# Half-height products side by side in a block's first product, and a planned first exchange, in a routed mixture of experts

## The chip, the core and the metric

The kernel runs on one core of one Trainium2 chip. The metric is the device time of one execution in microseconds (us), taken as the median of several runs; lower is better. TensorE (PE in the profile) multiplies, VectorE (DVE) and ScalarE (ACT) do element-wise work, GpSimd (POOL) and SyncE (SP) issue the transfers. A matmul needs its stationary operand loaded first, by an instruction of its own (LDWEIGHTS, PEld in the profile).

## What is computed

A causal convolution of 7 taps a head over 8 x 3584 tokens of 192 numbers, then a mixture of 8 experts in which each of the N = 28672 tokens goes to the one expert with the highest logit:

```python
x = _attn_ref(x, weight).reshape(B * S, D)          # D = 192
xn = x / (np.linalg.norm(x, axis=-1, keepdims=True) + 1e-06)
en = emb / (np.linalg.norm(emb, axis=-1, keepdims=True) + 1e-06)
logits = xn @ en.T / tau
expert_idx = np.argmax(logits, axis=1)
gate_w = softmax(logits)[np.arange(N), expert_idx]
for e in range(8):
    mask = expert_idx == e
    h = np.maximum(x[mask] @ w1[e], 0.0)            # 192 -> 1024
    out[mask] = gate_w[mask, None] * (h @ w2[e])    # 1024 -> 192
```

## The kernel before

Numbers are held as two f16 parts, a high one and a low one, and a product is the sum of high x high, low x high and high x low.

**The head** (`head`, planned by `_Plan`) loads and splits the weights of the eight experts (`weights`, where `low` on DVE writes the low parts, line L437, from what `high` on ACT wrote, L432), convolves and routes the first two chunks of 1792 tokens and convolves the third (`chunk`, line L529). `_Plan` is a list scheduler: `P.add(engine, us, emit, *after)` adds a step with a guessed duration, and `run` emits the steps in the order of the earliest possible start. What it emits on PE, DVE and ACT keeps that order. A step's `lag` is added for a follower on another engine.

**Routing.** The other chunks are convolved (`mix`, L761), routed (`route`) and their rows scattered to per-expert lists in DRAM, piece by piece in between the blocks (`dispatch`, driven by `run`). `run` holds the next piece in `live`; it is None once every chunk has been routed.

**Blocks** (`expert`). A block is up to 512 tokens of one expert, fetched transposed (`fetch`, a DMA into `e_xT`, and a small one into `e_mt`). The 192 inputs stand in `e_xT` as three groups of 128 rows: k = 0 the high parts of inputs 0 to 127, k = 2 their low parts, and k = 1 the high parts of inputs 128 to 191 on rows 0 to 63 and their low parts on rows 64 to 127. The exchange (`flip`, L1128, two DVE copies into `e_xf`) makes from k = 1 a group k = 3 whose halves are swapped. `copy_w1` (L1088) and `copy_w2` (L1091) copy the block's weights into `slot`.

The first product (L1161) makes 8 chunks of 128 hidden values. A bank of the accumulator holds m = 512 / T chunks of a block of T tokens, so T = 512 takes 8 banks, T = 256 takes 4 and T = 128 takes 2. Each chunk takes five whole matmuls:

```python
for i, (o, k) in enumerate(
        ((0, 0), (0, 2), (1, 0), (2, 1), (2, 3))):
```

Here o names the weights: 0 and 1 the high and low ones for inputs 0 to 127, 2 both parts for inputs 128 to 191, which stand high over low for the first four chunks and low over high for the last four. The pair (2, 1) and (2, 3) together gives the three wanted products of inputs 128 to 191 and one more, low x low. Each finished bank is read by ACT (L1165, relu, the high part `hh`) and then by DVE (L1167, the low part `hl`). The second product (L1189) takes 24 matmuls of 192 columns for every 128 tokens, then ACT scales the result (L1194) and POOL scatters it to the output (L1196).

The eight banks are in three rings, `h` with 5, `r` with 2 and `l` with 1; both products use `h`, and the other two serve the routing. The scheduler of the framework may reorder instructions where no dependency holds them; `_dep(..., False)` pins an order without a wait.

Of the kernel before, what the change touches and what calls it, by code (L numbers as in the profile page):

```python
# [40 lines left out]
NFC = F // 128  # L41
# [21 lines left out]
LATE = 1.0  # L63
PICKED = 5.0
ACTS = 8, 10, 16
LAND_X, LAND_T = 9.0, 6.0
TURN, FETCH, PIECE = 5.1, 2.1, 1.4
RANK_L, RANK_P = 2.0, 1.5
STEP1, STEP2, STEPC, STEPL = 1.08, 1.98, 0.65, 0.62
# [63 lines left out]
def _dep(tc, frm, to, sync=True):  # L133
    cls = mybir.DependencyClass.Sync if sync else mybir.DependencyClass.NoSync
    tc.add_manual_dep(
        frm, to, mybir.DependencyInfo(cls, mybir.DependencyReason.DATA),
        reason="routed rows are written before they are read",
    )


class _Moe:
    def __init__(self, ctx, tc, x, weight, emb, tau, w1, w2, out):
# [38 lines left out]
        self.xts, self.mixed = [], {}  # L181
        self.clk, self.gated, self.mm = 0.0, False, None
        self.asked, self.sp_at, self.low, self.parts = {}, 0.0, None, []
        self.chosen = {}
        self.subs, self.ready, self.flips, self.at, self.copied = [], 0, 0, 0, 0


    def ps(self, ring, shape, dt, name):
        n = 2048 // (2 if dt == F16 else 4)
        t = self.rings[ring].tile([128, n], dt, tag=ring, name=name)  # L190
        w = int(np.prod(shape[1:]))
        v = t[: shape[0], :w]
        if len(shape) == 3:
            v = v.rearrange("p (a b) -> p a b", b=shape[2])
        elif len(shape) == 4:
            v = v.rearrange("p (a b c) -> p a b c", b=shape[2], c=shape[3])
        return v
# [941 lines left out]
    def expert(self):  # L1139
# [13 lines left out]
            "p (c t) -> p c t", t=T) for i in range(2))  # L1153

        m = 512 // T
        for b in range(0, NFC, m):
            ps = self.ps("h", [128, m, T], F32, "h_ps")
            for c in range(m):
                for i, (o, k) in enumerate(
                        ((0, 0), (0, 2), (1, 0), (2, 1), (2, 3))):  # L1160
                    self.mm = nc.tensor.matmul(  # L1161
                        out=ps[:, c, :], lhsT=w1(o, b + c), rhs=xk[k],
                        start=(i == 0), stop=(i == 4)).ins
                    self.tick(STEP1 / (5 * m), self.mm)
            self.step = nc.scalar.activation(  # L1165
                out=hh[:, b:b + m, :], in_=ps, func=AF.Relu).ins
            self.low = nc.vector.scalar_tensor_tensor(  # L1167
                out=hl[:, b:b + m, :], in0=ps, scalar=0.0, in1=hh[:, b:b + m, :],
                op0=ALU.max, op1=ALU.subtract).ins
            if b == (0 if m > 2 else 2 if m == 2 else 1) and u == 0:  # L1170
                self.copy_w2()
            if m == 4:
                self.copy_w1(self.at, (b // 4,))
            yield self.slack(512)
# [5 lines left out]
            scalar1=self.slot[:, WS:RES].bitcast(F32), scalar2=None, op0=ALU.mult)  # L1180
        terms = sum(([(hh, c, k) for c in range(b, b + m) for k in (0, D)]
                     + [(hl, c, 0) for c in range(b, b + m)]
                     for b in range(0, NFC, m)), [])
        for a in range(nj):
            self.next_out = self.clk + STEP2 + EVICT
            o = self.ps("h", [128, D], F32, "o_ps")
# [73 lines left out]
    def head(self, first):  # L1260
# [35 lines left out]
            self.subs += sum(self.pick(128, first, most=MORE), [])  # L1296

        n = p = P.add("DVE", 3.8, pick, ranked[-1], pri=PICKED)
        for _ in range(3):
            n = P.add("SP", 2.0, lambda: self.fetch(), n, *sent, at)  # L1300
        n = P.add("DVE", 1.3, lambda: self.copy_w1(0), p,
                  *[v for l in low for v in l[:3]])
        P.add("DVE", 4.2, more, n, *[l[3] for l in low], pri=2.0)
        P.run()
        self.asked = {c: -LAND_X for c in range(4)}
        self.sp_at = 0.0
# [37 lines left out]
    def run(self):  # L1344
# [21 lines left out]
        while live or self.pend or not done or self.at < len(self.subs):  # L1366
# [16 lines left out]
            else:  # L1383
# [2 lines left out]
                self.clk += 0.5  # L1386
                if live:
                    live = next(a, None)
            if not live and not done and not self.pend:
                self.last_blocks()  # L1390
                done = True
# [27 lines left out]
```

## Time and profile before

| what | value |
|---|---|
| median of 3 runs | 1187.54 us (1187.27 to 1188.91) |
| profiled execution, its own time | 1184.81 us |
| profiled execution, span first to last instruction | 1183.1 us |
| PE busy | 1118.7 us, 95% of the span |
| DVE, ACT, POOL busy | 73%, 50%, 46% |
| mean granted clock of TensorE | 0.965 |

The 1.7 us between the span and its execution's time lie around the instructions. Matmuls are pipelined: a record's end is modelled and reaches past the start of the next one, so the cost of a matmul in a stream is read from start to start. The granted clock is 1.0 at 2.4 GHz and 0.5 at 1.2 GHz.

### The profile page before, as it was taken

How to read it: one execution, taken by the hardware profiler on the slowest of the kernel's cores; microseconds unless marked ns; L12 is line 12 of the kernel's file. 1: busy time of each engine (PE TensorE's matmuls, PEld its weight loads, DVE VectorE, ACT ScalarE, POOL GpSimd, SP SyncE). 2: the span in 40 equal slices, each digit the busy share in tenths (PEclk: the TensorE clock that was granted, in tenths of full speed). 3: DMA queues.
4: the chain of work that ended last, by engine and by line, in shares of the span. 5: the costliest groups of instructions: out<-in, count | busy, mean ns of one | idle time of the engine just before them, and what ended most of it. 6: DMA issues, size and time to landing. Idle time of an engine off the chain costs nothing. (4 is left out here: it accounts for less than half of the span.)

```text
span 1183.1 us, 29407 instructions
## 1 busy us (share of the span) xinstructions
PE 1118.7 (95%) x10732; PEld 911.5 (77%) x10732; DVE 866.3 (73%) x2314; ACT 592.3 (50%) x1354; POOL 546.5 (46%) x538
## 2 busy tenths in 40 slices
PE   5736999999999999999999999999999999999998
PEld 3633887889888898678967676776677777889997
DVE  5996998787978889768797676755447456467775
ACT  5867856364635546456464554434433334333333
POOL 1273245747555574655756556465552222222222
PEclk9556999999999999999999999999999999999999
DMA  9762355747365474764754756353222112112220
GB/s 276 232 217 53 81 109 131 164 96 160 74 149 135 116 166 98 156 133 94 176 111 125 147 112 122 79 124 80 70 70 56 39 45 53 44 42 48 49 49 28
DMA packets 267365, 127.50 MB, mean 108 GB/s; under 512 B 208671, under 2 KB 257182, under 8 KB 267217
## 3 DMA queue, kind: packets, MB, share of 16 engines
q1 hardware_dynamic: 243536, 78.71, 31.6%
q0 software_dynamic: 23664, 46.87, 13.9%
q8 instruction: 86, 1.41, 0.5%
q14 instruction: 63, 0.51, 0.2%
q10 hardware_dynamic: 16, 0.01, 0.0%
HBM read 38.35 MB, written 47.24 MB: 72 GB/s over the span
## 5 line engine op out<-in xcount | busy, mean ns | idle before, releaser
L1161 PE MATMUL h_ps<-e_xT,slot 128*128 128x256 f16 (+2 forms) x3136 | 496.5, 290 | 5.1 <-DVE slot L1088 4.8
L1189 PE MATMUL o_ps<-slot,hid 128*128 128x192 f16 x5472 | 481.8, 246 | 3.3 <-DVE hid L1167 2.2
L1189 PEld LDWEIGHTS <-hid 128*128 128x128 f16 x5472 | 453.7, 98 | 31.8 <-issue 9.4
L1161 PEld LDWEIGHTS <-slot 128*128 128x128 f16 x3920 | 345.5, 98 | 157.9 <-issue 10.9
L1196 POOL DMA_INDIRECT out_dram<-y,e_mt x228 | 252.7, 1108 | 437.2 <-ACT y L1194 409.7
L1167 DVE SCALAR_TENSOR_TENSOR hid<-h_ps,hid 128x512 f16<-128x512 f32 x456 | 309.2, 686 | 112.9 <-ACT hid L1165 110.7
L1165 ACT ACTIVATE hid<-h_ps 128x512 f16<-128x512 f32 x456 | 269.1, 597 | 199.3 <-PE h_ps L1161 192.1
L972 POOL DMA_INDIRECT rows_d<-rows,di x256 | 277.3, 1083 | 144.9 <-PE h_ps L1161 40.0
L1194 ACT ACTIVATE y<-o_ps,g 128x192 f32<-128x192 f32 x228 | 95.0, 420 | 305.8 <-PE o_ps L1189 271.6
L1161 PE MATMUL h_ps<-e_xf,slot 128*128 128x256 f16 (+2 forms) x784 | 217.8, 291 | 0.0
L1091 DVE COPY slot<-res 128x3074 f16 x98 | 96.6, 986 | 131.2 <-PE o_ps L1189 125.8
L1088 DVE COPY slot<-res 128x3072 f16 (+1 forms) x119 | 96.4, 810 | 1.2 <-issue 0.6
L761 PE MATMUL conv_ps<-xt,band 128*112 128x384 f32 x208 | 84.5, 498 | 0.0
L766 ACT COPY xt<-conv_ps 112x384 f32<-112x384 f32 x104 | 49.3, 479 | 31.5 <-PE conv_ps L761 30.8
L1128 DVE COPY e_xf<-e_xT 64x256 f16<-64x256 f16 (+2 forms) x196 | 46.1, 235 | 17.7 <-DMA e_xT<-rows_d 13.6
L773 ACT ACTIVATE sq<-xt 112x192 f32<-112x192 f32 x156 | 55.5, 361 | 1.8 <-DVE sq L777 0.7
L808 ACT CAST rows<-xt 112x768 f16<-112x768 f32 x56 | 46.1, 832 | 11.7 <-DVE xt L806 4.5
L806 DVE TENSOR_TENSOR xt<-xt,x_p_s 112x768 f32<-112x768 f32 x56 | 51.6, 950 | 0.2
L843 PEld LDWEIGHTS <-xT 128*112 128x112 f16 x672 | 44.0, 132 | 7.8 <-DMA xT<-rows 3.1
L843 PE MATMUL lg_ps<-ma,xT 128*112 128x16 f16 x448 | 43.8, 193 | 2.1 <-DMA xT<-rows 1.8
L810 DVE TENSOR_TENSOR rows<-xt,rows 112x512 f16<-112x512 f32 x56 | 38.4, 686 | 5.8 <-ACT rows L808 5.6
L843 PE MATMUL lg_ps<-mb,xT 128*112 128x16 f16 x224 | 37.7, 196 | 0.3 <-ACT xT L838 0.3
(212 smaller groups left out, 644.2 us busy)
## 6 DMA issues: line engine op xcount, KB each, us to landing
xt<-in_dram SPq DMA_DIRECT2D x42, 384.0 KB
res<-in_dram SPq DMA_DIRECT2D x6, 768.0 KB
rows_d<-rows,di POOLq DMA_INDIRECT x256
out_dram<-y,e_mt POOLq DMA_INDIRECT x228
xT<-rows SPq DMA_TRANSPOSE x208
res<-in_dram SPq DMA_DIRECT2D x6, 512.0 KB
xt<-in_dram SPq DMA_DIRECT2D x2, 1536.0 KB
xt<-in_dram SPq DMA_DIRECT2D x2, 1440.0 KB
```

The costliest lines, as they stand in the source:

```text
L761: i = nc.tensor.matmul(out=ps, lhsT=self.band[:, h, :], rhs=xt[:, :, h * G:(h + 1) * G], start=True, stop=True).ins
L773: self.over(nc.scalar.activation(out=sq, in_=xc[:, t, :], func=AF.Square, accum_out=n2[:, t:t + 1]).ins)
L843: i = nc.tensor.matmul(out=lg[:, g * GX + a, :], lhsT=xT[:, a, k, :], rhs=self.mb if k == 1 else self.ma, start=(k == 0), stop=(k == 2)).ins
L972: i = self.nc.gpsimd.indirect_dma_start(out=self.rows_d[:, :], out_offset=bass.IndirectOffsetOnAxis(ap=idx, axis=0), in_=src, in_offset=No ...
L1088: self.under(nc.vector.tensor_copy(out=o, in_=v).ins)
L1091: self.nc.vector.tensor_copy(out=self.slot[:, W2:], in_=self.res2[:, bass.ds(self.we, IMG)])
L1161: self.mm = nc.tensor.matmul(out=ps[:, c, :], lhsT=w1(o, b + c), rhs=xk[k], start=(i == 0), stop=(i == 4)).ins
L1165: self.step = nc.scalar.activation(out=hh[:, b:b + m, :], in_=ps, func=AF.Relu).ins
L1167: self.low = nc.vector.scalar_tensor_tensor(out=hl[:, b:b + m, :], in0=ps, scalar=0.0, in1=hh[:, b:b + m, :], op0=ALU.max, op1=ALU.subtrac ...
L1189: self.mm = nc.tensor.matmul(out=o, lhsT=h[:, c, q], rhs=w2[:, c, k:k + D], start=(n == 0), stop=(n == 3 * NFC - 1)).ins
L1194: self.step = nc.scalar.activation(out=y, in_=o, func=AF.Copy, scale=g[:, a:a + 1]).ins
L1196: i = nc.gpsimd.indirect_dma_start(out=self.out[:, :], out_offset=bass.IndirectOffsetOnAxis(ap=mt[:, a, 0:1], axis=0), in_=y, in_offset=No ...
```

## The change

It has two parts.

**Half-height products.** Once `live` is None (`routed`), blocks of 512 and 256 tokens take four whole matmuls a chunk, of which the fourth is (2, 3) for the first four chunks and (2, 1) for the last four; it gives low x high and high x low of inputs 128 to 191. What is left, high x high, is a matmul of 64 rows: for a chunk of the first half on rows 0 to 63 (`e_xT`), for one of the second half on rows 64 to 127 (`e_xf`). `sides` issues these in pairs, one of each half, into two banks. All pairs of a block stand together behind the first two banks' whole matmuls (behind the first bank's at T = 256), and open the remaining banks. The banks are taken in the order first half, second half, and so are the terms of the second product. `ps` now gives out all eight banks in turn, and each matmul of these blocks is pinned behind the one before (`mul`). The program has 14 such blocks of 512 tokens and 8 of 256, with 56 and 32 pairs. Blocks of 128 tokens, and all blocks before, keep five matmuls a chunk.

**The first exchange.** In `head` the exchange of block 0 becomes a step of the plan, behind `copy_w1` and all low parts of the weights, with a lag of 3.0 us behind the first fetch; `more`, the selection of three small blocks, comes behind it.

```diff
-LAND_X, LAND_T = 9.0, 6.0
+LAND_X, LAND_T, LAND_E = 9.0, 6.0, 3.0
...
     def ps(self, ring, shape, dt, name):
         n = 2048 // (2 if dt == F16 else 4)
+        if self.routed and ring == "h":
+            self.bank += 1
+            ring = "hhrhhrhl"[self.bank % 8]
...
+        order = range(0, NFC, m)
+        if self.routed and m <= 2:
+            order = [v for b in range(0, NFC // 2, m) for v in (b, b + NFC // 2)]
+        banks, half = {}, NFC // 2
+
+        def mul(b, c, o, x, p=slice(0, 128), start=False, stop=False):
+            i = nc.tensor.matmul(
+                out=banks[b][:, c, :], lhsT=w1(o, b + c)[p], rhs=x[p],
+                start=start, stop=stop, skip_group_check=True).ins
+            if self.mm is not None:
+                _dep(tc, i, self.mm.name, False)
+            self.mm = i
+            self.tick(STEP1 / (5 * m), i)
...
+        def full(b):
+            new = b not in banks
+            if new:
+                bank(b)
             for c in range(m):
                 for i, (o, k) in enumerate(
-                        ((0, 0), (0, 2), (1, 0), (2, 1), (2, 3))):
...
+                        ((0, 0), (0, 2), (1, 0), (2, 3 if b < half else 1))):
+                    mul(b, c, o, xk[k], start=new and not c and not i,
+                        stop=not new and i == 3)
+
+        def sides():
+            old = set(banks)
+            for b in range(0, half, m):
+                for v in (b, b + half):
+                    if v not in old:
+                        bank(v)
+                for c in range(m):
+                    for v, k, p in ((b, 1, slice(0, 64)),
+                                    (b + half, 3, slice(64, 128))):
+                        mul(v, c, 2, xk[k], p, start=v not in old and not c,
+                            stop=v in old and c == m - 1)
+
+        for n, b in enumerate(order):
+            if self.routed and m <= 2:
+                if n < 2 // m:
+                    full(b)
+                    if n < 2 // m - 1:
+                        continue
+                    sides()
+                    ready = order[:n + 1]
+                else:
+                    full(b)
+                    ready = [b]
...
+        fetched = []
         for _ in range(3):
-            n = P.add("SP", 2.0, lambda: self.fetch(), n, *sent, at)
+            n = P.add("SP", 2.0, lambda: self.fetch(), n, *sent, at, lag=LAND_E)
+            fetched.append(n)
         n = P.add("DVE", 1.3, lambda: self.copy_w1(0), p,
                   *[v for l in low for v in l[:3]])
-        P.add("DVE", 4.2, more, n, *[l[3] for l in low], pri=2.0)
+        n = P.add("DVE", 0.5, self.flip, n, fetched[0], *[l[3] for l in low])
+        P.add("DVE", 4.2, more, n, pri=2.0)
         P.run()
...
                 if live:
                     live = next(a, None)
+            self.routed = not live
```

The order of the built programs shows three places. In the changed file the lines are shifted: L437 is L440, L1088 is L1091, L1091 is L1094, L1128 is L1131, L1189 is L1244; the whole matmuls of the changed blocks, their pairs and their LDWEIGHTS all have line L1165, that of `mul`.

**DVE at the end of the head, before.** `res_94` and `res_95` hold the experts' weights, `slot` and `hid` as sources the raw weights of the last two experts.

```order
L437 SCALAR_TENSOR_TENSOR res_94<-slot,w_p_s,res_94 128x1024
L1128 COPY e_xf<-e_xT 64x256 x2
L437 SCALAR_TENSOR_TENSOR res_94<-slot,w_p_s,res_94 64x512 x2
L437 SCALAR_TENSOR_TENSOR res_94<-hid,w_p_s,res_94 128x1024
L437 SCALAR_TENSOR_TENSOR res_94<-hid,w_p_s,res_94 64x512 x2
L1076 TENSOR_LOAD sel_3584_989
L1088 ISA
L1088 COPY slot<-res_94 128x3072
L437 SCALAR_TENSOR_TENSOR res_95<-slot,w_p_s,res_95 128x8x192
L437 SCALAR_TENSOR_TENSOR res_95<-hid,w_p_s,res_95 128x8x192
L1007 TENSOR_TENSOR sl_av<-cb_871,start 1x8
```

The same place now:

```order
L440 SCALAR_TENSOR_TENSOR res_94<-slot,w_p_s,res_94 128x1024
L440 SCALAR_TENSOR_TENSOR res_94<-slot,w_p_s,res_94 64x512 x2
L440 SCALAR_TENSOR_TENSOR res_94<-hid,w_p_s,res_94 128x1024
L440 SCALAR_TENSOR_TENSOR res_94<-hid,w_p_s,res_94 64x512 x2
L1079 TENSOR_LOAD sel_3584_989
L1091 ISA
L1091 COPY slot<-res_94 128x3072
L440 SCALAR_TENSOR_TENSOR res_95<-slot,w_p_s,res_95 128x8x192
L440 SCALAR_TENSOR_TENSOR res_95<-hid,w_p_s,res_95 128x8x192
L1131 COPY e_xf<-e_xT 64x256 x2
L1010 TENSOR_TENSOR sl_av<-cb_871,start 1x8
```

The exchange (COPY e_xf, two copies in one row) has moved from behind the first low part of expert 6 to behind the last low part of expert 7; five low parts, the copy of block 0's first weights and the two 128x8x192 low parts now stand ahead of it.

**PE in the first product of a routed 512 block, before.** h_ps_13393, 13401 and so on are banks in turn, e_xT and e_xf the block's inputs.

```order
L1161 MATMUL h_ps_13393<-e_xT_12909,slot_96 128x512
L1161 LDWEIGHTS slot_96
L1161 MATMUL h_ps_13393<-e_xT_12909,slot_96 128x512
L1161 LDWEIGHTS slot_96
L1161 MATMUL h_ps_13393<-e_xf_13347,slot_96 128x512
L1161 LDWEIGHTS slot_96
L1161 MATMUL h_ps_13401<-e_xT_12909,slot_96 128x512
L1161 LDWEIGHTS slot_96
L1161 MATMUL h_ps_13401<-e_xT_12909,slot_96 128x512
L1161 LDWEIGHTS slot_96
```

The same block now, from the last whole matmul of the second bank on; 13393 and 13398 are the first two banks, for chunks 0 and 4.

```order
L1165 MATMUL h_ps_13398<-e_xT_12909,slot_96 128x512
L1165 LDWEIGHTS slot_96
L1165 MATMUL h_ps_13393<-e_xT_12909,slot_96 128x512
L1165 LDWEIGHTS slot_96
L1165 MATMUL h_ps_13398<-e_xf_13347,slot_96 128x512
L1165 LDWEIGHTS slot_96
L1165 MATMUL h_ps_13406<-e_xT_12909,slot_96 128x512
L1165 LDWEIGHTS slot_96
L1165 MATMUL h_ps_13407<-e_xf_13347,slot_96 128x512
L1165 LDWEIGHTS slot_96
L1165 MATMUL h_ps_13410<-e_xT_12909,slot_96 128x512
L1165 LDWEIGHTS slot_96
```

The last two matmuls of before into one bank have become one whole matmul, and pairs of e_xT and e_xf into two banks each follow each other; the rows don't say that they are of 64 rows.

**PE from a 128 block into a 256 block, before.** o_ps_16959 is the 128 block's second product, of 24 matmuls; h_ps_17005 and 17018 are the first banks of the 256 block.

```order
L1189 MATMUL o_ps_16959<-slot_96,hid_99 128x192
L1161 LDWEIGHTS slot_96
L1161 MATMUL h_ps_17005<-e_xT_16694,slot_96 128x256
L1161 LDWEIGHTS slot_96
L1161 MATMUL h_ps_17005<-e_xT_16694,slot_96 128x256
...
L1161 MATMUL h_ps_17018<-e_xT_16694,slot_96 128x256
L1189 LDWEIGHTS hid_99
L1189 MATMUL o_ps_16959<-slot_96,hid_99 128x192
L1189 LDWEIGHTS hid_99
...
L1161 MATMUL h_ps_17005<-e_xf_16989,slot_96 128x256
```

The same place now:

```order
L1244 LDWEIGHTS hid_99
L1244 MATMUL o_ps_16959<-slot_96,hid_99 128x192
L1165 LDWEIGHTS slot_96
L1165 MATMUL h_ps_17005<-e_xT_16694,slot_96 128x256
L1165 LDWEIGHTS slot_96
L1165 MATMUL h_ps_17005<-e_xT_16694,slot_96 128x256
L1165 LDWEIGHTS slot_96
L1165 MATMUL h_ps_17005<-e_xT_16694,slot_96 128x256
L1165 LDWEIGHTS slot_96
L1165 MATMUL h_ps_17005<-e_xf_16989,slot_96 128x256
L1165 LDWEIGHTS slot_96
```

Before, eight matmuls of the next block that read e_xT stood ahead of the last four of the second product, and e_xf was first read after sixteen matmuls of the block. Now the second product runs through and e_xf is read by the fourth.

## Rows read from the trace of the kernel before

**Rows 1.** The page, part 1: busy time of each engine.

```profile
PE 1118.7 (95%) x10732; PEld 911.5 (77%) x10732; DVE 866.3 (73%) x2314; ACT 592.3 (50%) x1354; POOL 546.5 (46%) x538
```

**Rows 2.** Stages of 20 us: length, busy (x instructions) of PE, PEld, DVE, ACT, POOL, clock, DMA, GB/s.

```profile
120.00:140.00 20.00, 19.60 (x215) 17.15 (x213) 19.68 (x64) 18.14 (x57) 5.84 (x6) 1.00 0.44 90
820.00:840.00 20.00, 20.00 (x154) 13.38 (x153) 10.29 (x17) 8.38 (x16) 10.58 (x12) 1.00 0.29 74
```

**Rows 3.** Waits of PE from 110 us on: total us, times, longest.

```profile
PE h_ps L1161 <- DVE slot L1088: 4.8, 3, 3.5
PE o_ps L1189 <- DVE hid L1167: 2.2, 3, 1.7
```

**Rows 4.** Timeline, end of the head: start, us, engine, what, [idle before it <- releaser].

```profile
94.61 1.28 DVE L437 SCALAR_TENSOR_TENSOR res<-slot,w_p_s,res 128x1024 f16<-128x1024 f32 x1 [0.34 <-ACT res L432]
...
99.96 1.56 ACT L432 ACTIVATE res<-hid,w_p_s 128x1536 f16<-128x1536 f32 x1
...
105.12 0.46 DVE L1128 COPY e_xf<-e_xT 64x256 f16<-64x256 f16 x2 [9.22 <-DMA e_xT<-rows_d]
...
105.50 1.52 DVE L437 SCALAR_TENSOR_TENSOR res<-slot,w_p_s,res 64x512 f16<-64x512 f32 x2
105.91 1.49 PE L761 MATMUL conv_ps<-xt,band 128*112 128x384 f32 x2
...
107.05 2.84 DVE L437 SCALAR_TENSOR_TENSOR res<-hid,w_p_s,res 128x1024 f16<-128x1024 f32 x3
...
109.93 0.96 DVE L1088 COPY slot<-res 128x3072 f16 x1
...
110.94 0.61 PE L1161 MATMUL h_ps<-e_xT,slot 128*128 128x256 f16 x4 [3.55 <-DVE slot L1088]
```

**Rows 5.** Stages of 1 us at the end of the head, columns as in rows 2.

```profile
107.00:108.00 1.00, 0.40 (x1) 0.00 (x0) 0.97 (x2) 1.00 (x6) 0.00 (x0) 0.50 0.37 49
108.00:109.00 1.00, 0.00 (x0) 0.00 (x0) 0.97 (x2) 0.61 (x4) 0.00 (x0) 0.94 0.13 16
...
111.00:112.00 1.00, 1.00 (x8) 0.82 (x9) 1.00 (x1) 0.00 (x0) 0.00 (x0) 0.76 0.03 8
112.00:113.00 1.00, 1.00 (x5) 0.72 (x4) 1.00 (x2) 0.23 (x1) 0.00 (x0) 0.50 0.00 0
...
114.00:115.00 1.00, 1.00 (x7) 0.73 (x5) 1.00 (x3) 0.89 (x4) 0.00 (x0) 0.53 0.00 0
```

**Rows 6.** Timeline of PE in the first routed 512 block, columns as in rows 4.

```profile
798.47 1.03 PE L1161 MATMUL h_ps<-e_xT,slot 128*128 128x512 f16 x4
...
807.10 8.08 PE L1189 MATMUL o_ps<-slot,hid 128*128 128x192 f16 x96
815.02 1.03 PE L1161 MATMUL h_ps<-e_xT,slot 128*128 128x512 f16 x4
```

**Rows 7.** Timeline of PE in a 256 block.

```profile
1155.32 0.60 PE L1161 MATMUL h_ps<-e_xT,slot 128*128 128x256 f16 x4
...
1155.98 0.60 PE L1161 MATMUL h_ps<-e_xT,slot 128*128 128x256 f16 x4
```

**Rows 8.** Groups of instructions by form: busy us, mean ns of one, idle before, releasers.

```profile
L1167 DVE SCALAR_TENSOR_TENSOR hid<-h_ps,hid 128x512 f16<-128x512 f32 x456 | 309.2, 686 | 112.9 <-ACT hid L1165 110.7
...
L1165 ACT ACTIVATE hid<-h_ps 128x512 f16<-128x512 f32 x456 | 269.1, 597 | 199.3 <-PE h_ps L1161 192.1 <-DVE slot L1091 1.0 <-DVE hid L1167 0.7
...
L1091 DVE COPY slot<-res 128x3074 f16 x98 | 96.6, 986 | 131.2 <-PE o_ps L1189 125.8 <-issue 5.2
...
L1161 PE MATMUL h_ps<-e_xf,slot 128*128 128x512 f16 x216 | 79.2, 379 | 0.0
```

**Rows 9.** Timeline from a 128 block into a 256 block.

```profile
1150.14 1.85 PE L1189 MATMUL o_ps<-slot,hid 128*128 128x192 f16 x20
...
1151.15 0.68 DVE L1167 SCALAR_TENSOR_TENSOR hid<-h_ps,hid 128x512 f16<-128x512 f32 x1
...
1152.33 0.46 DVE L1128 COPY e_xf<-e_xT 64x256 f16<-64x256 f16 x2
```

More of the change, by code (lines that the diff above doesn't have):

```diff
@@ L183, in __init__ @@
         self.asked, self.sp_at, self.low, self.parts = {}, 0.0, None, []
-        self.chosen = {}
+        self.chosen, self.routed, self.bank = {}, False, 0
         self.subs, self.ready, self.flips, self.at, self.copied = [], 0, 0, 0, 0
@@ L1155, in expert @@
         m = 512 // T
-        for b in range(0, NFC, m):
-            ps = self.ps("h", [128, m, T], F32, "h_ps")
+        order = range(0, NFC, m)
[10 more added lines that the diff above has]
+            self.tick(STEP1 / (5 * m), i)
@@ L1158, in expert, with bank @@
+        def bank(b):
+            banks[b] = self.ps("h", [128, m, T], F32, "h_ps")
+        def full(b):
+            new = b not in banks
+            if new:
+                bank(b)
             for c in range(m):
                 for i, (o, k) in enumerate(
-                        ((0, 0), (0, 2), (1, 0), (2, 1), (2, 3))):
-                    self.mm = nc.tensor.matmul(
-                        out=ps[:, c, :], lhsT=w1(o, b + c), rhs=xk[k],
-                        start=(i == 0), stop=(i == 4)).ins
@@ L1164, in expert @@
[L1164 to L1170, printed above, removed]
+                        ((0, 0), (0, 2), (1, 0), (2, 3 if b < half else 1))):
@@ new lines, in expert @@
+        for n, b in enumerate(order):
[9 more added lines that the diff above has]
+                    ready = [b]
+            else:
+                bank(b)
+                for c in range(m):
+                    for i, (o, k) in enumerate(
+                            ((0, 0), (0, 2), (1, 0), (2, 1), (2, 3))):
+                        self.mm = nc.tensor.matmul(
+                            out=banks[b][:, c, :], lhsT=w1(o, b + c), rhs=xk[k],
+                            start=(i == 0), stop=(i == 4)).ins
+                        self.tick(STEP1 / (5 * m), self.mm)
+                ready = [b]
+            for v in ready:
+                self.step = nc.scalar.activation(
+                    out=hh[:, v:v + m, :], in_=banks[v], func=AF.Relu).ins
+                self.low = nc.vector.scalar_tensor_tensor(
+                    out=hl[:, v:v + m, :], in0=banks[v], scalar=0.0,
+                    in1=hh[:, v:v + m, :], op0=ALU.max, op1=ALU.subtract).ins
+            if n == (0 if m > 2 else 1) and u == 0:
@@ L1182, in expert @@
                      + [(hl, c, 0) for c in range(b, b + m)]
-                     for b in range(0, NFC, m)), [])
+                     for b in order), [])
         for a in range(nj):
```

## The prediction

> **What bounds the kernel now.** I read the page first: PE is busy 1118.7 of 1183.1 us, the next engine, DVE, 866.3 [rows 1]. A share of the whole span hides stages, so next the stages of 20 us. Just behind the head, from 120 to 140 us, PE is busy 19.60, but DVE 19.68 and ACT 18.14: three engines are close together. Behind all routing, from 820 to 840 us, PE is busy all 20.00 at full clock and DVE only 10.29, ACT 8.38 [rows 2]. There whatever PE is spared should come off the time. Then PE's waits from 110 us on: the longest is 3.5 us, on DVE's copy into slot; the three waits of the second product on DVE's low parts are 2.2 us together [rows 3]. So from the first block on PE waits for little, and in the head it waits for DVE. The timeline of the end of the head says why: DVE has written the first low part of expert 6 at 94.61 + 1.28 = 95.89, and then idles 9.22 us for the landing of e_xT, because the exchange stands next in its order; only behind it come the five low parts that the copy of the first weights needs (1.52 and 2.84 us), then this copy at 109.93, and PE begins block 0 at 110.94, after 3.55 us of waiting for it [rows 4].
>
> **The planned exchange.** It is issued as before, two copies, but behind those parts. DVE goes on at 95.89: two low parts of 1.52 us, then three of 2.84 end at 100.3, the copy of 0.96 at 101.3; ACT's last high part ends at 99.96 + 1.56 = 101.5, so the two 128x1536 low parts end near 105. The row of 105.12 gives the landing: the exchange runs when it did before [rows 4]. So DVE is over 8 us ahead, the exchange is hidden behind nothing but the landing, and what is queued behind it (the selection of `more`, the copy of the second weights) moves forward with it. PE cannot use all that: two convolutions stand ahead of block 0 at 105.91 and their record ends at 107.4 [rows 4]. The first matmuls need e_xT (105.1) and slot (101.3), so they start at about 107.4: 3.55 us.
>
> There is a second gain in the same place. PE's clock reads 0.50 from 107 to 108 and 0.94 in the next us; PE then idles, block 0 starts at full clock at 110.94, and the clock falls to 0.76, 0.50, 0.50 (113 to 114 reads like the one before) and 0.53 in the four stages from 111 us on [rows 5]. The half-clock time in there is 0.48 + 1.00 + 1.00 + 0.94 = 3.4 us, which costs half of it, 1.7. Starting at 107.4, PE has half clock for 0.6 + 0.12 us, a cost of 0.36, and then no idle stretch ahead of a fall. Gain 1.35. Together **-4.9 us**. Bounds: 0, if DVE or ACT bind from 120 us on, and 3.55 + 1.7 = 5.3.
>
> **The half-height products.** In the first routed 512 block the first product runs from 798.47 to 807.10, 8.63 us for 40 matmuls, 0.2157 each; the second 7.92 us for 96 [rows 6]. In a 256 block six matmuls take 1155.98 - 1155.32 = 0.66, 0.11 each [rows 7]. The change leaves 32 whole matmuls and 4 pairs a block. No row shows two matmuls in the array at once. If a pair lasts as long as one matmul, a block of 512 saves 4 x 0.2157 = 0.863, a block of 256 saves 0.44: 14 x 0.863 + 8 x 0.44 = **-15.6 us**. If they run one after the other, a pair costs two and the saving is 0. I take the upper end: the two halves share no rows of the array and no bank, and a load of weights (PEld, 13.38 us busy in a stage where PE is busy 20.00 [rows 2]) fits twice into a pair of 512.
>
> The array has to be divided ahead of the pairs and made whole behind them, twice a block, 44 times. No row shows such a switch. At the lower end it costs nothing. For the price, I take the emptying of the array: a whole 512 matmul has a record of 379 ns [rows 8], but the next starts after 216 [rows 6]; the 163 ns between is what a matmul needs behind its last column. If nothing new enters in that time, 44 x 0.163 = **+7.2 us**. If a load of weights is laid open as well, some 0.1 us more, 11.6; that is the upper end. I take 7.2, the nearest row.
>
> The page "TensorEngine Tiling (Array Packing)" of the Trainium skill states, under Tiling Modes, that a change of the tiling mode, not only of the tile, drains the engine. It speaks against a free switch; no run here has shown it yet. The page "TensorE: Matmul & The Clock Gate", Part 3, gives starts 4 ns apart for matmuls in different row groups, but a measured 3.07 for four. By 3.07 / 4, an estimate, two would gain 1.54 and not 2, and a pair of 512 would last 0.28 us; the saving would be 11.0 in place of 15.6, and the sum -6.0 in place of -10.6. A rival of that kind is priced below, from rows.
>
> **What the fixed order costs.** From a 128 block into a 256 block, before, PE had twelve matmuls to do until the exchange was through. Now the second product runs through: 24 matmuls from 1150.14 at 0.0825 end at 1152.12, three matmuls on e_xT at 1152.45, and the fourth needs e_xf, which DVE finishes at 1152.33 + 0.46 = 1152.79 [rows 6, 7, 9]: 0.34 us of waiting at each of the 8 such blocks, **+2.7 us**. The last four of the 24 need the low part that ends at 1151.83 and start after 20, at 1151.79: nothing to 0.1 us. Bounds 0 and 3.6. Ahead of a 512 block three whole matmuls give 0.3 us more cover than ahead of a 256 one, so I put nothing there.
>
> **What stays hidden.** The copies, exchanges and transfers of a block are the same in number; DVE at 10.29 of 20 hides them. Two banks now are finished at once, behind 8 matmuls and 4 pairs, at 8 x 0.2157 + 0.88 = 2.6 us, the others every 0.863. DVE needs 0.686 a bank, ACT 0.597 [rows 8], so both keep up: the eight low parts end at about 2.6 + 0.6 + 8 x 0.686 = 8.7, or 0.7 + 0.6 behind the last bank at 7.9 with the switches, 9.2; the second product needs the last at 7.9 + 23 x 0.0825 = 9.8. Cover 0.6 us. All banks in turn means that the eighth reuses that of the last second product; it is opened 2.4 us later, and ACT reads it within one.
>
> **Sum.** -4.9 - 15.6 + 7.2 + 2.7 = -10.6 us. Against the profiled execution's own 1184.81 that is 1174.2; that execution was 2.7 us below the median of the runs, 1187.54, and I carry the difference to the median: **1176.9 us**.
>
> **Rivals.** (1) *The pairs run one after the other, and the switches cost.* Place: the eight half-height matmuls of a block. For it: no row shows two at once. Against: separate rows and banks. Then 0 + 7.2 + 2.7 - 4.9 = +5.0, 1192.5, slower. It decides from the point where less than 5.0 of the 15.6 us, a third of each pair's second matmul, is overlapped. (2) *One after the other and free switches*: -2.2, 1185.3. (3) *Pairs side by side and free switches*, the weights and columns of the next mode entering behind the last: -17.8, 1169.7. For it: in the stream, loads of weights already overlap the matmuls. (4) *The head's gain is given back*, because DVE at 19.68 and ACT at 18.14 of 20 [rows 2] bind behind it: -5.7, 1181.8. Against: DVE itself is over 8 us ahead. (5) *DVE becomes late for the second product*: if the copy of the second weights, 0.986 us [rows 8], falls between the low parts and not ahead of them, the cover of 0.6 turns into a wait of 0.4 in each of the 14 blocks of 512, +5.6: -5.0, 1182.5. Against: that copy waits only for the second product before, which has ended when the block begins. (6) *The halves overlap only in part*: the second of a pair starts behind its own load of weights, as the second product seems to run, at 0.0825 a matmul. A pair then lasts 0.298 us at 512 and 0.19 at 256, the saving is 14 x 0.53 + 8 x 0.11 = 8.4, and the sum -3.4, 1184.1. For it: a load stands between the two in the order. Against: in whole matmuls the load is hidden [rows 6].
>
> **Chances.** Forecast 0.46, own range 1173 to 1181 (a pair somewhat longer than one matmul, a switch from 0.07 to 0.25 us). (1) 0.08, (2) 0.06, (3) 0.16, (4) 0.09, (5) 0.06, (6) 0.09. About 0.2%, 2.4 us, can be told from no change here. Faster are the forecast and (3) to (6): 0.86; (2) is within it, 0.06; (1) slower, 0.08. The range 1168 to 1186 takes in all but (1) and the tails of free switches and of a dear one.
>
> **What would show it.** In the changed trace: block 0's first matmul at about 107.4 and no half clock behind 109; the exchange still at 105. In a routed 512 block the start of the first product to that of the second 8.63 - 0.86 + 0.33 = 8.1 us, near 4.1 at 256 for 4.4; in the pairs, records of e_xT and e_xf that start together. A first product of 8.6 or more means rival 1 or 2, of 7.8 rival 3. PE's waits would list e_xf by about 0.3 us eight times, and if rival 5 holds, hid in the second product. The forecast is wrong if PE's start in the head is set by something other than these two convolutions, or if a pair is worth much less than one whole matmul.

## The result, and the profile after

| what | before | after |
|---|---|---|
| median | 1187.4 us (1186.25 to 1188.91, 4 runs) | 1172.32 us (1170.1 to 1173.61, 4 runs) |
| profiled execution, its own time | 1184.81 us | 1172.65 us |
| profiled execution, span | 1183.1 us | 1170.9 us |

The ratio is 0.9868, 95% interval 0.985 to 0.9885: faster, by 15.1 us in the medians (1.3%). The forecast was 1176.9 with a range of 1168 to 1186, so the time lies inside, 4.6 us below the forecast. The narrower range that the prediction gave to its own mechanism, 1173 to 1181, it misses by 0.7 us.

The page, part 1, of the changed kernel answers to [rows 1]; PE has lost 10.4 us of busy time with as many matmuls:

```profile
PE 1108.3 (95%) x10732; PEld 898.3 (77%) x10732; DVE 868.3 (74%) x2314; ACT 592.0 (51%) x1354; POOL 550.0 (47%) x538
```

Two stretches tell where the time went: from the last group of matmuls on the weight totals (`n_ps`, in the head, ahead of both edits) to the first routed block, and from there to the end. Stages of before, columns as in rows 2:

```profile
92.38:798.47 706.09, 692.22 (x6545) 564.62 (x6545) 557.52 (x1594) 381.57 (x958) 390.04 (x371) 0.99 0.55 122
798.47:1183.10 384.63, 378.93 (x3826) 308.56 (x3824) 232.56 (x463) 145.18 (x274) 120.51 (x119) 1.00 0.21 52
```

The same stages of the changed kernel:

```profile
93.98:794.87 700.89, 690.44 (x6545) 564.20 (x6546) 557.79 (x1594) 380.66 (x958) 388.47 (x371) 0.99 0.56 122
794.87:1170.90 376.03, 369.86 (x3826) 295.98 (x3824) 234.35 (x463) 145.81 (x274) 125.60 (x119) 1.00 0.21 53
```

The first stretch is 5.2 us shorter, the second 8.6. What lies ahead of them differs by 1.6 us the other way (93.98 against 92.38), and -5.2 - 8.6 + 1.6 is the 12.2 us between the two profiled executions. That of before was 2.6 us below its median, that of after 0.3 above; the rest of the 15.1 is in there.

The first routed 512 block, PE's timeline of the changed kernel (columns as in rows 4), answers to [rows 6]:

```profile
794.87 0.81 PE L1165 MATMUL h_ps<-e_xT,slot 128*128 128x512 f16 x3
795.51 0.38 PE L1165 MATMUL h_ps<-e_xf,slot 128*128 128x512 f16 x1
795.73 1.35 PE L1165 MATMUL h_ps<-e_xT,slot 128*128 128x512 f16 x5
796.69 0.39 PE L1165 MATMUL h_ps<-e_xf,slot 64*128 64x512 f16 x1
796.92 0.38 PE L1165 MATMUL h_ps<-e_xT,slot 64*128 64x512 f16 x1
796.92 0.38 PE L1165 MATMUL h_ps<-e_xf,slot 64*128 64x512 f16 x1
...
797.35 0.38 PE L1165 MATMUL h_ps<-e_xT,slot 64*128 64x512 f16 x1
797.35 0.38 PE L1165 MATMUL h_ps<-e_xf,slot 64*128 64x512 f16 x1
797.66 0.82 PE L1165 MATMUL h_ps<-e_xT,slot 128*128 128x512 f16 x3
...
802.85 3.38 PE L1244 MATMUL o_ps<-slot,hid 128*128 128x192 f16 x39
```

The two halves of a pair start together (2 to 4 ns apart in each of the 88 pairs of the trace), and the next pair about 0.216 us later (796.69 to 797.35 are three pitches, 0.22 each), as whole matmuls follow one another. The fifth instruction in the row of 795.73 is the first pair's half on e_xT (its record ends where its partner's does, at 797.08). Four whole matmuls from 795.73 would be through at 796.59, but the pair begins at 796.69; the last pair at 797.35 would be through at 797.57, but the next whole matmul begins at 797.66. Those two gaps of about 0.10 us are the switches. The first product is 802.85 - 794.87 = 7.98 us, where it was 8.63 [rows 6]: 36 x 0.2157 = 7.77, and 0.21.

The loads of weights (PEld) in the same place of the changed kernel show what stands in the gaps:

```profile
796.69 0.55 PEld L1165 LDWEIGHTS <-slot 64*128 64x128 f16 x8 [0.42 <-issue]
797.66 4.86 PEld L1165 LDWEIGHTS <-slot 128*128 128x128 f16 x24 [0.42 <-issue]
```

Within a run of whole matmuls a load starts 0.21 us ahead of its own matmul, beside the one before. At a switch it does not: the first load behind each of the 44 switches starts 4 to 5 ns ahead of its matmul, and its record is 92 to 97 ns long, about as long as the gap.

From a 128 block into a 256 block, timeline of DVE and PE of the changed kernel, answers to [rows 9]:

```profile
1152.55 0.49 PE L1165 MATMUL h_ps<-e_xT,slot 128*128 128x256 f16 x3
1152.58 0.46 DVE L1131 COPY e_xf<-e_xT 64x256 f16<-64x256 f16 x2
1153.09 0.27 PE L1165 MATMUL h_ps<-e_xf,slot 128*128 128x256 f16 x1
...
1156.90 0.33 PE L1244 MATMUL o_ps<-slot,hid 128*128 128x192 f16 x2
```

Three matmuls of 0.108 are through at 1152.87, the one on e_xf begins at 1153.09: 0.22 us of waiting for the exchange, which ends at 1153.04. The list of waits does not show it, since the modelled ends of the records cover it; one sees it from start to start only. The first product is 4.35 us. Added up from start to start, those of all 8 such blocks take 34.92 us, before 34.93.

The end of the head in the changed kernel, timeline of all engines, answers to [rows 4]:

```profile
96.21 2.85 DVE L440 SCALAR_TENSOR_TENSOR res<-slot,w_p_s,res 128x1024 f16<-128x1024 f32 x3 [0.34 <-ACT res L435]
98.62 1.25 POOL L975 DMA_INDIRECT rows_d<-rows,di  x1 [0.31 <-issue]
...
101.50 1.55 POOL L975 DMA_INDIRECT rows_d<-rows,di  x1 [0.30 <-issue]
101.97 0.96 DVE L1091 COPY slot<-res 128x3072 f16 x1
...
105.12 1.33 SPq L1109 DMA_TRANSPOSE e_xT<-rows_d  x1
107.15 0.92 PE L764 MATMUL conv_ps<-xt,band 128*112 128x384 f32 x2
108.23 0.45 DVE L1131 COPY e_xf<-e_xT 64x256 f16<-64x256 f16 x2 [1.84 <-DMA e_xT<-rows_d]
108.34 0.92 PE L1214 MATMUL h_ps<-e_xT,slot 128*128 128x256 f16 x7 [0.27 <-DMA e_xT<-rows_d]
```

DVE no longer idles ahead of the low parts, and block 0 begins at 108.34 with a wait of 0.27 for e_xT in place of 3.55 for DVE [rows 4]. Counted from the start of the `n_ps` group (93.98; 92.38 before) it begins after 14.36 us where it was 18.56. The stages of 1 us there, which answer to [rows 5], show that the clock is up when it begins and stays up:

```profile
107.00:108.00 1.00, 1.00 (x3) 0.29 (x1) 0.00 (x0) 0.58 (x2) 0.00 (x0) 0.82 0.78 150
108.00:109.00 1.00, 0.73 (x8) 0.62 (x8) 0.73 (x4) 1.00 (x6) 0.00 (x0) 1.00 0.06 1
...
111.00:112.00 1.00, 1.00 (x8) 0.66 (x7) 0.86 (x7) 1.00 (x6) 0.00 (x0) 1.00 0.17 29
...
114.00:115.00 1.00, 1.00 (x9) 0.63 (x7) 0.40 (x2) 1.00 (x6) 0.00 (x0) 1.00 0.00 0
```

PE's waits from 110 us on, of the changed kernel, answer to [rows 3]: the wait for slot is gone, that for DVE's low parts is 2.6 us in place of 2.2; those for row loads (2.9, where it was 1.8) and for `e_xT` are longer.

```profile
PE lg_ps L846 <- DMA xT<-rows: 2.9, 5, 1.1
PE o_ps L1244 <- DVE hid L1222: 2.6, 4, 1.7
PE h_ps L1214 <- DMA e_xT<-rows_d: 1.0, 1, 1.0
```

### The profile page after: what moved, and what is told of

It is laid out like the page before. It is cut to its first block, busy times and chain, and to the rows that moved or that the text cites. A ratio compares the mean times of both kernels' runs of the same rounds, so it can differ in the third digit from the quotient of the medians.

```text
span 1170.9 us, 29417 instructions
## 1 busy us (share of the span) xinstructions
PE 1108.3 (95%) x10732; PEld 898.3 (77%) x10732; DVE 868.3 (74%) x2314; ACT 592.0 (51%) x1354; POOL 550.0 (47%) x538
## 4 chain that ended last, share of the span: by engine, by line
PE 53%; issue 21%; POOL 9%; DVE 7%; DMA 7%; ACT 2%; SPq 1%; POOLq 0%; DVEq 0%; ACTq 0%
PE h_ps L1214 23%; PE o_ps L1244 20%; POOL out_dram L1251 7%; PE conv_ps L764 5%; PE lg_ps L846 3%; DMA out_dram<-y,e_mt 3%; POOL rows_d L975 2%; DMA xT<-rows 1%; DVE res L440 1%; SPq L971 1%; DMA rows_d<-rows,di 1%; PE conv_ps L532 1%; DMA e_xT<-rows_d 1%; DVE xt L616 1%; DMA band<-cseq_d 0%
## 5 line engine op out<-in xcount | busy, mean ns | idle before, releaser
L1244 PE MATMUL o_ps<-slot,hid 128*128 128x192 f16 x5472 | 480.4, 247 | 3.4 <-DVE hid L1222 2.6
L1244 PEld LDWEIGHTS <-hid 128*128 128x128 f16 x5472 | 453.4, 98 | 30.8 <-issue 9.7
L1214 PE MATMUL h_ps<-e_xT,slot 128*128 128x256 f16 (+2 forms) x2432 | 346.5, 276 | 1.5 <-DMA e_xT<-rows_d 1.3
L1214 PEld LDWEIGHTS <-slot 128*128 128x128 f16 x3040 | 259.4, 98 | 88.5 <-issue 11.4
L1094 DVE COPY slot<-res 128x3074 f16 x98 | 96.5, 985 | 118.2 <-PE o_ps L1244 117.5
L1214 PE MATMUL h_ps<-e_xf,slot 128*128 128x256 f16 (+2 forms) x608 | 164.3, 276 | 0.1
L1165 PE MATMUL h_ps<-e_xT,slot 128*128 128x512 f16 (+3 forms) x704 | 145.7, 341 | 0.0
L1165 PEld LDWEIGHTS <-slot 128*128 128x128 f16 (+1 forms) x880 | 73.4, 97 | 69.6 <-issue 17.5
L1091 DVE COPY slot<-res 128x3072 f16 (+1 forms) x119 | 96.7, 812 | 0.9 <-issue 0.7
L1131 DVE COPY e_xf<-e_xT 64x256 f16<-64x256 f16 (+2 forms) x196 | 46.2, 236 | 9.8 <-DMA e_xT<-rows_d 5.7
L1165 PE MATMUL h_ps<-e_xf,slot 128*128 128x512 f16 (+3 forms) x176 | 48.8, 340 | 0.5
```

Source lines behind the costliest of these rows:

```text
L1091: self.under(nc.vector.tensor_copy(out=o, in_=v).ins)
L1094: self.nc.vector.tensor_copy(out=self.slot[:, W2:], in_=self.res2[:, bass.ds(self.we, IMG)])
L1165: i = nc.tensor.matmul(out=banks[b][:, c, :], lhsT=w1(o, b + c)[p], rhs=x[p], start=start, stop=stop, skip_group_check=True).ins
L1214: self.mm = nc.tensor.matmul(out=banks[b][:, c, :], lhsT=w1(o, b + c), rhs=xk[k], start=(i == 0), stop=(i == 4)).ins
L1244: self.mm = nc.tensor.matmul(out=o, lhsT=h[:, c, q], rhs=w2[:, c, k:k + D], start=(n == 0), stop=(n == 3 * NFC - 1)).ins
```

## The experiments

The theory after this reading: head -5.2 us; pairs -15.6 (they last as one matmul), switches about +4.5 (44 at 0.10), fixed order about +2 in the routed stretch. The main rival: pairs and switches are not two opposite terms, but the new order itself, eight banks in turn and nothing else, is what gains. Each experiment is the changed kernel but for the edit shown. Runs e1 to e4 were timed against a before of 1188.8 us, e5 to e8 against 1189.05. The two stretches of each profiled execution:

| kernel | n_ps to first routed block | from there to the end | median us | ratio to before (95%) |
|---|---|---|---|---|
| before | 706.09 | 384.63 | 1187.4 | |
| changed | 700.89 | 376.03 | 1172.32 | 0.9868 (0.985 to 0.9885) |
| e1, head alone | 701.56 | 384.62 | 1181.95 | 0.9943 (0.9924 to 0.9962) |
| e2, pairs alone | 708.97 | 376.15 | 1179.81 | 0.9921 (0.99 to 0.9942) |
| e3, sides whole | 699.79 | 387.04 | 1182.82 | 0.9951 (0.9932 to 0.9971) |
| e4, split runs | 704.25 | 383.69 | 1182.18 | 0.9936 (0.9913 to 0.9958) |
| e5, e_xf last | 700.61 | 374.27 | 1170.4 | 0.9852 (0.983 to 0.9874) |
| e6, 512 alone | 703.19 | 376.07 | 1173.59 | 0.9873 (0.9853 to 0.9893) |
| e7, early runs | 701.59 | 374.27 | 1169.01 | 0.9834 (0.9814 to 0.9854) |
| e8, early all | 695.58 | 374.22 | 1163.86 | 0.9801 (0.9775 to 0.9826) |

The second column of times moves only with edits to the routed blocks (384.63 and 384.62, 376.03 and 376.15, 374.27, 374.27 and 374.22), so it can be read to 0.1 us. The first cannot. Changed, e1, e3, e4, e5 and e6 have the same program there and spread from 699.79 to 704.25; before and e2, the same as each other, take 706.09 and 708.97. So only the means of such groups tell something: 701.7 with the planned exchange, 707.5 without it. Part of the spread is the clock: near 330 us PE waits for row loads, and then the granted clock reads 0.50 for 3.4 us in six of the ten executions, for 6.8 us in all in e6 and e8, and not at all in e4 and e7, which costs 1.7, 3.4 and 0 us. The stages of 50 us around it in e5, e7 and e8, columns as in rows 2:

```profile
292.89:342.94 50.05, 48.17 (x484) 42.83 (x483) 38.58 (x112) 23.89 (x62) 28.08 (x27) 0.97 0.56 122
292.99:343.11 50.12, 48.15 (x492) 42.68 (x489) 38.32 (x109) 24.60 (x63) 28.39 (x28) 1.00 0.59 121
292.44:342.12 49.68, 46.74 (x460) 39.46 (x459) 36.09 (x106) 22.91 (x60) 29.34 (x26) 0.93 0.54 113
```

**e1, the planned exchange alone.**

```diff
-            self.routed = not live
+            self.routed = False
```

> Only the planned exchange; blocks keep five whole matmuls a chunk and the five h banks. Theory: the exchange alone gives 4.9 to 5.2 us, 1182.3 us; first block's first product about 14.4 us behind the last weight totals' matmul (18.6 before), and 700.9 us from there to the first routed block (706.1 before). Rival: the 5 us were chance of one execution or are given back behind the head, 1187 us.

1181.95 us, 6.9 below before (interval 4.5 to 9.0). The routed stretch is as before:

```profile
92.52:794.08 701.56, 690.75 (x6544) 564.52 (x6545) 557.92 (x1594) 380.98 (x958) 387.75 (x371) 0.99 0.55 122
794.08:1178.70 384.62, 378.93 (x3826) 308.57 (x3824) 232.49 (x463) 145.19 (x274) 120.60 (x119) 1.00 0.21 52
```

The head's gain is there by itself, 4.5 us in the trace, and DVE and ACT don't take it back behind the head (rival 4). Block 0 begins 14.81 us behind `n_ps` here, not 14.4 as expected: the clock is still at 0.50 from 107 to 108, the convolutions take as long as before, and PE begins block 0 behind them without a listed wait:

```profile
107.33 2.34 PE L1214 MATMUL h_ps<-e_xT,slot 128*128 128x256 f16 x16
```

```profile
107.00:108.00 1.00, 1.00 (x5) 0.48 (x4) 0.97 (x3) 1.00 (x6) 0.00 (x0) 0.50 0.25 50
```

**e2, the half-height products alone.** The five lines of the head as in before:

```diff
-        fetched = []
...
-            n = P.add("SP", 2.0, lambda: self.fetch(), n, *sent, at, lag=LAND_E)
-            fetched.append(n)
+            n = P.add("SP", 2.0, lambda: self.fetch(), n, *sent, at)
...
-        n = P.add("DVE", 0.5, self.flip, n, fetched[0], *[l[3] for l in low])
-        P.add("DVE", 4.2, more, n, pri=2.0)
+        P.add("DVE", 4.2, more, n, *[l[3] for l in low], pri=2.0)
```

> Only the half-height pairs; the exchange as before. Theory: the routed stretch is 8.6 us shorter, 1178.8 us, and DVE idles some 9 us again for the landing in the head; the scatters at the end of the head take 0.94 us again as they did before, and not up to 1.55. Rival, most of the gain is in the head: 1183 us or more.

1179.81, 9.0 below before (interval 6.9 to 11.9); 6.85 and 8.99 make 15.8, against 15.1 for both together: the parts add up within their intervals. In its trace block 0 again begins 18.56 us behind n_ps (111.84 - 93.28), after 4.47 us of waiting for slot, with clock 0.50 from 110 to 116:

```profile
111.84 1.03 PE L1214 MATMUL h_ps<-e_xT,slot 128*128 128x256 f16 x4 [4.47 <-DVE slot L1091]
```

Its first stretch is 2.9 us longer than that of before, where the two programs are the same. PE's waits for row loads (`lg_ps` on `xT`) are 5.1 us there, 1.8 in before, enough to account for it.

**e3, the same order with whole sides.** Both matmuls of each pair over all 128 rows, so one after the other and no division of the array. The low x low product comes back, as in before.

```diff
-                    for v, k, p in ((b, 1, slice(0, 64)),
-                                    (b + half, 3, slice(64, 128))):
+                    for v, k, p in ((b, 1, slice(0, 128)),
+                                    (b + half, 3, slice(0, 128))):
```

> The change, but every half-height matmul takes all 128 rows (the fifth product is whole again, low x low comes back), so same order, same eight banks, same pins, no two in the array at once and no switch. Theory: the gain of the routed stretch is the pairs': first product 8.63 us in a 512 block again, total 1184 us (5.2 from the exchange, about 2 lost to the pinned order). Rival: the eight banks and the new order gave the gain, and it stays near 1172 us.

1182.82, and the routed stretch is 387.04: 2.4 us longer than before, not shorter. So the order gains nothing by itself and costs 2.4 (2.7 forecast), and the pairs with their switches are worth 387.04 - 376.03 = 11.0 us. If a pair lasts as one matmul, which the starts above show, that is -15.6, and 4.6 us are left for 44 switches, 0.104 each, the gap seen in the timeline.

**e4, more switches.** The pairs in three runs a 512 block (two pairs, one and one) and in two a 256 block: the same matmuls, and 14 x 4 + 8 x 2 = 72 more switches.

```diff
-        def sides():
+        def sides(at):
             old = set(banks)
-            for b in range(0, half, m):
+            for b in at:
...
-                    sides()
+                    sides([0])
...
+                    if b < half and b:
+                        sides([b])
                     full(b)
```

> The change, but a block's pairs in three runs and not one (two runs at 256 tokens): 72 switches more in all. Theory, each switch costs about 0.1 us: first product 8.4 us in a 512 block for 7.98, total +7.4, 1179.7 us. Rival, the 0.21 us above 36 matmuls are paid once a block (opening banks, waits): 1172 us, first product 8.0.

1182.18, 9.9 above the changed kernel's median. Of that, 1.4 is that the before of these runs was slower; by the two ratios to before it is 8.1. The routed stretch is 383.69, so 7.66 us more than 376.03: 0.106 us a switch, as in e3 and in the gaps. The timeline of its first routed block shows one more of them, 0.10 behind a run of two pairs (799.76 + 0.216 = 799.97, next at 800.07):

```profile
799.76 0.38 PE L1165 MATMUL h_ps<-e_xT,slot 64*128 64x512 f16 x1
799.76 0.38 PE L1165 MATMUL h_ps<-e_xf,slot 64*128 64x512 f16 x1
800.07 0.82 PE L1165 MATMUL h_ps<-e_xT,slot 128*128 128x512 f16 x3
```

What is left lies within the spread of the first stretch, where the programs are the same (704.25 against 700.89; row loads waited for 5.4 us in place of 2.9). The rival, by which the order gains, is out with e3 and e4.

**e5, e_xf last in a 256 block.** In the first bank both chunks' matmuls on e_xT go ahead of the two on e_xf:

```diff
-            for c in range(m):
-                for i, (o, k) in enumerate(
-                        ((0, 0), (0, 2), (1, 0), (2, 3 if b < half else 1))):
-                    mul(b, c, o, xk[k], start=new and not c and not i,
-                        stop=not new and i == 3)
+            last = [3] if new and m == 2 else []
+            for c, i in ([(c, i) for c in range(m) for i in range(4)
+                          if i not in last]
+                         + [(c, i) for c in range(m) for i in last]):
+                o, k = ((0, 0), (0, 2), (1, 0), (2, 3 if b < half else 1))[i]
+                mul(b, c, o, xk[k], start=new and not c and not i,
+                    stop=not new and i == 3)
```

> The changed kernel, but in the first chunks of a paired 256-token block the two matmuls on the flipped copy e_xf come behind the six on e_xT. Theory: in the changed kernel these blocks stand 0.21 to 0.27 us at their first e_xf matmul, at each of 8 changes from a 128-token to a 256-token block; six matmuls of 0.108 us take 0.65 us where three take 0.32, and the copy is done 0.54 us behind the first one, so the wait goes. Expected from the first routed block to the end 374.2 us (376.03 in the changed kernel, less 8 x 0.23), and 1170.5 us in all; before is at 1187 to 1189. Rival: the gap is no wait for e_xf but the change of array shape itself, which then comes a little later: 376 us for the stretch, 1172.3 in all.

The routed stretch is 374.27 (374.2 expected), the median 1170.4. The gap is gone: six matmuls from 1149.45 end at 1150.10, and there the one on e_xf begins.

```profile
1149.45 0.82 PE L1165 MATMUL h_ps<-e_xT,slot 128*128 128x256 f16 x6
1150.10 0.38 PE L1165 MATMUL h_ps<-e_xf,slot 128*128 128x256 f16 x2
1150.42 0.28 PE L1165 MATMUL h_ps<-e_xT,slot 64*128 64x256 f16 x1
```

So 1.76 us of the 2.4 that the fixed order costs are this wait, 0.22 at each of 8 blocks. The other 0.6 can be seen when the instructions of before and e3 are added up from start to start: 0.2 in the first products of 512 blocks (8.65 to 8.71 us in five of them, for 8.63), and 0.4 in the second products of 128 blocks. Five of these take 2.09 us in place of 1.98, with two gaps, behind their eighth and their twentieth matmul; the second opens 0.06 us behind the end of DVE's last low part.

**e6, pairs in 512 blocks alone.**

```diff
-        if self.routed and m <= 2:
+        if self.routed and m <= 1:
...
-            if self.routed and m <= 2:
+            if self.routed and m <= 1:
```

> The changed kernel with pairs in 512-token blocks alone; the 8 blocks of 256 tokens behind all routing are computed as before. Theory: a 256-token block's pairs give 0.44 us, and pay two switches at 0.104 us and a wait of 0.23 to 0.3 us for e_xf, so that 8 blocks gain between 0 and 0.6 us or lose 0.6. Expected from the first routed block to the end 375.4 to 376.2 us (376.03 in the changed kernel), 1171.7 to 1172.5 in all. Rival: the 256-token blocks hold their share of the gain (8 x 0.44 = 3.5 us): 379.5 us for the stretch, 1175.8 in all.

376.07 for the routed stretch, 0.04 from the changed kernel: the 256 blocks, 32 of the 88 pairs, gained nothing. (The median, 1173.59, is 1.3 above that of the changed kernel, from the first stretch, 703.19.) With e5 they gain 376.07 - 374.27 = 1.8 us, 0.225 a block: 0.43 of matmuls less two switches.

**e7, 512 blocks beside the routing too.** On top of e5, in two runs of two pairs, so that four banks of the ring of five are open at most:

```diff
-        if self.routed and m <= 2:
+        pair = self.routed and m <= 2 or m == 1
+        runs = 1 if self.routed else 2
+        if pair:
...
-        def sides():
+        def sides(first=0, end=None):
             old = set(banks)
-            for b in range(0, half, m):
+            for b in range(first, end or half, m):
...
-            if self.routed and m <= 2:
+            if pair and runs == 2:
+                full(b)
+                if b in (0, 2):
+                    sides(b, b + 2)
+                ready = [b]
+            elif pair:
```

> With the matmuls on e_xf last, and the 13 blocks of 512 tokens that stand beside the routing take pairs too, in two runs of two pairs each, within their five banks (29 runs with the three that other matmuls break). Theory: 13 x 0.863 = 11.2 us off, 58 switches at 0.104 = 6.0 us on, and 1.8 us off for e_xf: 1172.3 - 7.0 = 1165.3 us, all of the 5.2 in the stretch from the weight totals to the first routed block (700.9 us in the changed kernel, whose other runs spread by 2 us on either side, with waits for row loads). Rival: that stretch is held by the row loads and the evictions, so that PE only waits longer: 1170.5 us, as with e_xf last alone; slower than that if VectorE comes late with four of the five banks open.

1169.01: 1.4 below e5, where 5.2 were expected of PE's work. The first stretch took 701.59, against 700.61 in e5. In it PE is busy 685.63 us, against 689.78, but 1.7 of these 4.2 is the half clock near 330 us that e7 does not have. From start to start the first products of the 512 blocks take 109.0 us, against 112.2: 3.2 of the 5.2 came off. PE's idle time rose from 10.8 to 16.0. The intervals of e5 and e7 overlap, so that e7 is the faster one is not shown:

```profile
92.54:794.13 701.59, 685.63 (x6544) 553.92 (x6545) 557.70 (x1594) 381.27 (x958) 388.72 (x371) 0.99 0.55 122
```

**e8, 256 blocks beside the routing too.** On top of e7, one run of four pairs in each of these 41 blocks:

```diff
-        pair = self.routed and m <= 2 or m == 1
-        runs = 1 if self.routed else 2
+        pair = m <= 2
+        runs = 2 if m == 1 and not self.routed else 1
```

> As the run with two runs of two pairs, and the 41 blocks of 256 tokens beside the routing take pairs as well, in one run of four pairs (44 runs with the broken ones). Theory: a further 41 x 0.44 = 18.0 us off and 88 switches at 0.104 = 9.2 us on, so 8.9 less: 1156.4 us, if a flipped copy is there in time and no bank is waited for. Rival: with four of five banks open at once, and VectorE busy at 0.6 to 0.9 beside the routing, PE waits for banks or the second product for its low parts; a wait of 0.3 us a block (12 us) leaves it at 1168 or above, and slower than the run with the 512-token blocks alone.

1163.86, 5.1 below e7 where 8.9 were expected, and the fastest of all: 2.0% below before, 0.7% below the changed kernel by the medians.

```profile
93.70:789.28 695.58, 681.30 (x6545) 534.32 (x6545) 555.71 (x1594) 380.39 (x958) 394.94 (x371) 0.99 0.57 123
```

From start to start, added up over the timeline of this stretch, the first products of the 256 blocks take 181.7 us in e5 and 173.0 in e8 (-8.7, for -8.9 expected), those of the 512 blocks 112.2 and 108.6 (-3.6, for -5.2). The routing's logits (`lg_ps`) take 36.2 and 42.1, where the executions with one program range from 36.2 (e5) to 40.1 (e4): PE waits longer for the transposed rows. In e5 and in e8:

```profile
PE lg_ps L846 <- DMA xT<-rows: 2.8, 4, 1.6
```

```profile
PE lg_ps L846 <- DMA xT<-rows: 5.2, 10, 0.8
```

Both sides were half right in e7 and e8: of the 14.1 us expected of both edits together 12.3 came off the first products, but only 6.5 off the median. Longer waits show where some of the rest went: 2.4 us more of waits for the transposed rows, 1.0 for `e_xT` (1.9 us in e8, 0.9 in e5), 1.1 for VectorE's low parts in the second product (3.3 us, 2.2 in e5), and 1.7 more of half clock. That earlier loads would bring it back was not tried. The list of waits has PE waiting for a bank twice, in one 512 block, 0.8 us in e7 and 0.7 in e8:

```profile
PE h_ps L1167 <- DVE hid L1231: 0.7, 2, 0.5
```

## Why the prediction was right, and what it mis-sized

**The planned exchange**, forecast -4.9: measured -5.2 in the stretch, -4.5 in e1, -5.8 between the means of the eight executions above with and without it, and 6.9 us between the medians of e1 and before. So the size is right to some 2 us and not better. DVE ran ahead as worked out, no half clock stands behind 108 (0.82 and 1.00 in the rows above, against [rows 5]), and rival 4 is out. One reading was wrong: the exchange does not run when it did before. Less the 1.6 us by which the whole head came later, it stands at 106.6 and not at 105.1, because `e_xT` is issued 1.4 us later. And it was not the convolutions that set PE's start (0.27 us of waiting for `e_xT`, at 106.7 in the time of before, where 107.4 was said): they end sooner, since the clock rises within them. The two errors cancel, which is luck. In e1 the clock rose later, and there the convolutions did set the start, as forecast.

**The pairs**, -15.6: right. The halves start 2 to 4 ns apart and a pair has the pitch of one whole matmul, so rivals 1, 2 and 6 are out. The Trainium skill, "TensorE: Matmul & The Clock Gate", Part 3, gives starts about 4 ns apart for matmuls in different row groups, but a gain of 3.07 with four; here two gave the whole 2, apart from the switches.

**The switches**, +7.2: the step that was mis-sized. The sum priced a switch at 0.163 us, the time between a matmul's last column and the end of its record; three readings give 0.10 (gaps in the timeline 0.09 to 0.10, e3 0.104, e4 0.106), so 4.6 us. A switch does not wait for the end of the record: the pair of 796.69 begins before the modelled end of the whole matmul ahead of it (796.38 + 0.38 = 796.76). The price is neither free (rival 3) nor that of the row. The upper end had the emptying and a load of weights laid open one behind the other; the trace does show the load laid open, and it is about as long as the whole gap. Whether the gap is this load, the emptying of the array, or both at the same time, no run separates. "TensorEngine Tiling (Array Packing)" of the Trainium skill, Tiling Modes, says that changing the mode drains the engine; a gap at every change agrees with that, but no row shows the draining itself.

**The fixed order**, +2.7: 2.4 in e3, but not by the forecast's one term. The wait for e_xf is 0.22 us and not 0.34, as the exchange ends 0.49 us behind the block's first matmul and not 0.67; that makes 1.8. The other 0.6 are two terms put at nothing, the low part that the end of a second product needs (0.4) and the 512 blocks (0.2). That the total comes so near is luck.

**What stays hidden**: DVE kept up in the routed blocks; waits on its low parts are 2.6 us in place of 2.2, and rival 5 would have made 5.6 more.

**The sum**: -10.6 forecast, -13.8 measured in the two stretches. Of the 3.2 between them 2.6 are the switches, 0.3 the fixed order and 0.3 the head. The other 1.4 of the 4.6 us by which the forecast missed the median is how the two profiled executions, and the 1.6 us ahead of the stretches, stand to their medians. The head's 0.3 is less than its stretch spreads. The lengths given for a routed block, 8.1 and 4.1 us, were 7.98 and 4.35. The 4.1 does not follow from the sum's own terms, by which a 256 block would take 4.4 - 0.44 + 0.33 + 0.34 = 4.6, longer than before; it left out the wait and part of the switches.

## What to carry to other kernels

Here matmuls of 64 rows in the two halves of the array took the time of one, and each change between the whole and the divided array cost 0.10 us at both lengths, so what counts is how many pairs stand in a run: eight halves of 512 columns returned 0.86 us for 0.21, of 256 columns 0.43 for 0.21, and one wait of 0.22 us ate that. A fixed order that moves the use of a late operand forward should be read start to start, as modelled ends hide gaps below a record's length. In a stage that waits for loads, work taken off PE came back only in part (6.5 of 14.1 us in e8).

## What the runs showed of the hardware that was not expected

VectorE's work beside GpSimd's indirect DMAs made these longer. The last four scatters in the head of before, with DVE idle for all but the first 0.3 us of them, took 1.07, 0.94, 0.94 and 0.94 us, those of e2 1.08, 0.94, 0.94 and 0.94; in the changed kernel and in e1, e3 and e4, where DVE writes low parts at that time, they took 1.07 to 1.08, 1.25 to 1.26, 1.00 to 1.01 and 1.55. Of before:

```profile
95.63 1.07 POOL L972 DMA_INDIRECT rows_d<-rows,di  x1 [0.30 <-issue]
97.01 0.94 POOL L972 DMA_INDIRECT rows_d<-rows,di  x1 [0.30 <-issue]
```

That is 1.0 us of the 1.4 by which `e_xT` was issued later. The page "SBUF — State Buffer" of the Trainium skill, "A bandwidth-pool intuition that's wrong", has a DMA issued by GpSimd blocked by a DVE copy until about 115 ns behind the copy's end. The longest scatter agrees: the copy into slot ends at 101.97 + 0.96 = 102.93, the scatter at 101.50 + 1.55 = 103.05. For the other scatters no run shows which instruction held them.
